# The last 64 rows of w_down on TensorE's row halves in all four token blocks, with the turned rest on the whole array

## The chip, the cores and the metric

The kernel runs on one core of a Trainium2 chip. The metric is the device time of one execution in microseconds (us). TensorE (PE) multiplies matrices into eight banks of PSUM, VectorE (DVE), ScalarE (ACT) and GpSimd (POOL) do the rest, and SP issues the transfers. Each engine works off its own queue in order; a semaphore holds an instruction back until what it needs is there.

## The reference

2048 tokens x of width 640 go through two branches, and a gate per token mixes them. Cut to what matters:

```python
qkv = x @ wqkv                          # 32 heads of 20
pq, pk = q @ w_phi, k @ w_phi           # per head
phi = concat(softmax(p), softmax(-p))   # of pq and of pk
num = phi_q @ (phi_k.T @ v); den = phi_q @ sum(phi_k) + 1e-6
a = (num / den) @ wo
b = (silu(x @ w_gate) * (x @ w_up)) @ w_down      # w_gate, w_up: 640x1728, w_down: 1728x640
g = sigmoid((x * gate_w).sum(-1))
out = g * a + (1 - g) * b
```

The inner width 1728 of branch b is 13 x 128 + 64. The 64 rows left over are the subject of the change.

## The kernel before

**Blocks and steps.** Tokens are cut into 16 tiles of 128 and four blocks (bt 0 to 3) of 512. Branch b goes through a block in 14 steps k (`ffn`, L706): five matmuls of 512 columns for gate and five for up, each into a bank of its own; then `ffn_tail` (L672): ScalarE takes tanh of gate (L699), ScalarE copies up to `us` (L700), VectorE multiplies (L687), GpSimd makes the product (L697) into `hT`, which holds 14 steps of a block, for two blocks in turn. Step 13 has only 64 rows: its gate and its up share the two halves of the partitions of one bank, in one group of matmuls called gu.

**The sums (w_down).** `down` (L906) sums columns 0 to 511 of the result for one token tile: `hT` of a step stands still in the array, `wd` moves, and 14 matmuls of 512 columns add up in one bank. The last 128 columns are summed turned: in `rest` (L871) `wd` stands still, the block's 512 tokens move, 14 matmuls of 512 columns; ScalarE copies that and a transposing DMA turns it back.

**Block 3 is different (EDGE = (3,), L39).** Blocks 0 to 2 treat step 13 like the others: rows 64 to 127 of `hT`'s step 13 are zero (memset, L606), and a whole matmul is spent on 64 rows of use. In block 3, gu is ten matmuls of 256 columns, which lay the first 256 tokens of step 13 on partitions 0 to 63 and the last 256 on partitions 64 to 127 (the tail then works by halves: L676). `wd` has the 64 rows twice, once on each half (L595, L596). An **edge** (`edge`, L839) adds step 13 for all five sums with matmuls of 64 rows, taking the upper and the lower half in turn; the sums themselves have 13 steps. EARLY (L765) says which sums run ahead of the edge (they open their banks, and the edge closes them); for the others the edge opens the banks and the sum closes them. There the turned rest lies in a pair of banks, 256 tokens each, as 26 matmuls of 256 columns.

**Branch a.** Each key tile (`ktile`, L1119; `features`, L1026) multiplies into a pair of banks and one more for values, and VectorE passes over the pair four times (max L1077, min L1081, subtractions L1085 and L1089) before it is free; then exp, a sum, a reciprocal and GpSimd's product (L1110). Each query tile does the same in one bank, and then num, den, a transpose and the matmuls with `wo` (wof, worest: L1224, L1234).

**The order of the work.** `_Plan` (L253) decides it when the kernel is built: each task has an engine, a guessed cost, what it depends on, what it takes (banks and other buffers) and a priority. The planner goes through modelled time, lets each engine take the first task in its list whose needs are met, and writes the instructions in that order. Key tiles (3), query tiles (5), num, wo and worest (1 to 1.6) go ahead of branch b (10 and up). Within branch b the order is the list `seq` (L1268 to L1278): the sums of a block are strewn one by one among the steps of the next block from its sixth on (D_AFTER, L763), or behind them. K_AT, K_EACH, Q_AT and Q_EACH (L758) are the earliest times of key and query tiles. On the chip the written order is kept, whatever the real times are.

Of the kernel before, what the change touches and what calls it, by code (L numbers as in the profile page):

```python
# [38 lines left out]
EDGE = (3,)  # L39
# [318 lines left out]
def _build(  # L358
# [36 lines left out]
    wd = sb("wd", [P, NK, D], BF16)  # L395
    wg = sb("wg", [P, 5, F_FFN + 128], BF16)
# [109 lines left out]

    L_SLACK, E_SLACK, O_SLACK = 1.0, 1.8, 1.6
# [55 lines left out]
    def load_head(key, c0, c1, k0, k1, land, prio):  # L563
        w, src = (wg, gsrc) if key == "g" else (wu, usrc)
        t = load("sp", w[:, c0:c1, k0 * P:k1 * P], src[:, c0:c1, k0 * P:k1 * P], land, prio)
        for k in range(k0, k1):
# [29 lines left out]
            load("sp", wd[64:P, 13, :], B_w_down[13 * P:F_FFN, :], 59.3, -23.9)]  # L596
# [9 lines left out]
    add("dve", 0.5, lambda: memset(hT[64:P, :, 13, :], 0.0, "dve"), prio=-18)  # L606
# [65 lines left out]
    def ffn_tail(bt, k, ctx, last, n_after):  # L672
        hb = bt % 2
        halves = [(0, P, 0, P, slice(0, 512))]
        if k == 13:
            halves = [(r0, r0 + 64, 64 - r0, P - r0, slice(4 * r0, 4 * r0 + 256)) for r0 in (0, 64)] if bt in EDGE else [(0, 64, 64, P, slice(0, 512))]  # L676

        def each(fn):
            def go():
                for r0, r1, u0, u1, tk in halves:  # L680
                    fn(hT[r0:r1, hb, k, 0:tk.stop - tk.start], lambda: one(ctx["g"], 0, 512, r0, r1)[:, tk],
                       lambda: one(ctx["u" if k < 13 else "g"], 0, 512, u0, u1)[:, tk], lambda: us[r0:r1, ctx["us"], 0:tk.stop - tk.start])
            return go

        def stt(h, g, u, s_):
            g_ = g()
            dveop(lambda: dve.scalar_tensor_tensor(out=h, in0=h, scalar=1.0, in1=g_, op0=ALU.add, op1=ALU.mult), [h, g_], [h])  # L687

        def copy(h, g, u, s_):
            o_, u_ = s_(), u()  # L690
            run("act", lambda: act.activation(o_, u_, ACTF.Copy, scale=0.5), reads=[u_], writes=[o_] if k < 13 else [o_, u_])  # L691

        def mult():
            n = 256 if k == 13 and bt in EDGE else 512
            r1 = 64 if k == 13 and bt not in EDGE else P
            h, u_ = hT[0:r1, hb, k, 0:n], us[0:r1, ctx["us"], 0:n]
            poolop(lambda: pool.tensor_tensor(h, h, u_, ALU.mult), [h, u_], [h])  # L697
        x_ = 0.15 if k == 13 and bt in EDGE else 0.0
# [4 lines left out]
        mult_t[bt, k] = add("pool", 0.6 if k == 13 and bt in EDGE else 1.11, mult,  # L703
                            deps=[t2, t3], prio=0, rel=[("us", ctx, "us")], name="hmul")

    def ffn(bt, k, rank):  # L706
# [68 lines left out]

    DM = 512
# [62 lines left out]
    def edge(bt, rank):  # L839
        hb = bt % 2  # L840
        c_ = down_c[bt] = {j: {} for j in range(-1, 4)}
        acq = [("pair" if j < 0 else "bank", c_[j], "ps") for j in range(-1, 4) if j not in EARLY[bt]] + ([("bank", c_[3], "p2")] if bt == NBT - 1 else [])

        def turned(r0):
            return (bank(c_[-1]["ps"], r0 // 64, 0, 256), wd[r0:r0 + 64, 13, DM:D], hT[r0:r0 + 64, hb, 13, 0:256], -1)
# [11 lines left out]
    def body(bt, j, o, pairs):  # L857
        if bt not in EDGE:
            return acc(o(), pairs)
        early = j in EARLY[bt]  # L860
        return [(o(), l, r, early and i == 0, not early and i == 12) for i, (l, r) in enumerate(pairs)]

    def sums(bt, j, cost, fn, rank, acq, name):
        if bt not in EDGE:
            t_ = add("pe", cost, fn, deps=[mult_t[bt, k] for k in range(NK)] + wd_l, prio=rank, acq=acq, name=name)
            return t_, t_
        t_ = add("pe", cost, fn, deps=[mult_t[bt, k] for k in range(13)] + wd_l, prio=rank, acq=acq if j in EARLY[bt] else (), name=name)
        (edge_t[bt] if j in EARLY[bt] else t_).deps.append(t_ if j in EARLY[bt] else edge_t[bt])
        return t_, edge_t[bt] if j in EARLY[bt] else t_

    def rest(bt, rank):  # L871
        ctx = down_c[bt][-1]
# [3 lines left out]
        got = [("pair" if bt in EDGE else "bank", ctx, "ps")]  # L876

        def fn():
            if bt not in EDGE:
                mms(acc(one(ctx["ps"], 0, 512), [(wd[:, k, DM:D], hT[:, hb, k, :]) for k in range(NK)]))  # L880
                return
            mms([g for i in range(2) for g in body(bt, -1, lambda i=i: bank(ctx["ps"], i, 0, 256),
                                                   [(wd[:, k, DM:D], hT[:, hb, k, 256 * i:256 * i + 256]) for k in range(13)])])
        rest_t[bt], r_ = sums(bt, -1, _mm(*([256] * 26 if bt in EDGE else [512] * 14)), fn, rank, got, "rest")

        def rcp():
            if bt not in EDGE:
                actop(xb[:, ctx["xb"], 0:512], one(ctx["ps"], 0, 512), ACTF.Copy)
                return
            i_ = wide(ctx["ps"], 1024).rearrange("p (i x) -> p i x", i=2)[:, :, 0:256]  # L890
            actop(xb[:, ctx["xb"], 0:512].rearrange("p (i x) -> p i x", i=2), i_, ACTF.Copy)
        e = add("act", 0.49, rcp, deps=[r_], prio=1, acq=[("xb", ctx, "xb")], rel=got, name="rcp")
# [13 lines left out]
    def down(bt, u, rank):  # L906
        t = 4 * bt + u
        ctx = down_c[bt][u]
        hb = bt % 2
        tk = slice(P * u, P * u + P)  # L910

        def part(key, c0, c1):
            return lambda: mms(body(bt, u, lambda: one(ctx[key], 0, c1 - c0), [(hT[:, hb, k, tk], wd[:, k, c0:c1]) for k in range(13 if bt in EDGE else NK)]))
        if t < NT - 1:
            down_t[bt, u], d_ = sums(bt, u, _mm(*[DM] * (13 if bt in EDGE else NK)), part("ps", 0, DM), rank, [("bank", ctx, "ps")], "down")
            return t, ctx, [(d_, "ps", 0, DM)]
        assert u not in EARLY[bt]
        first, _ = sums(bt, u, _mm(*[384] * 13), part("ps", 0, 384), rank, (), "down")
        second = add("pe", _mm(*[128] * 13), part("p2", 384, DM), prio=0.0, name="down")
        second.after = first  # L920
        down_t[bt, u] = second
        return t, ctx, [(first, "ps", 0, 384), (second, "p2", 384, DM)]
# [344 lines left out]
    late = downs_of(NBT - 2)[LATE:]  # L1267
    seq = [("f", k, bt) for k in range(K_PAIRS) for bt in range(2) if bt or k >= HD]  # L1268
    seq += [("f", k, 0) for k in range(K_PAIRS, NK)]
    for bt in range(1, NBT):  # L1270
        ks = list(range(K_PAIRS if bt == 1 else 0, NK))
        ds = downs_of(bt - 1)
        for i, k in enumerate(ks):
# [4 lines left out]
    seq = [e for e in seq if e not in late] + late + downs_of(NBT - 1)  # L1278
    downs = []
    for i, (kind, j, bt) in enumerate(seq):  # L1280
        if kind == "f":
            ffn(bt, j, 10.0 + 0.01 * i)
        elif kind == "d":
            if bt in EDGE and bt not in edge_t:
                edge(bt, 10.0 + 0.01 * seq.index(("x", 0, bt)))
            down_c.setdefault(bt, {c: {} for c in range(-1, 4)})
            if j < 0:
                rest(bt, 10.0 + 0.01 * i)
                continue
# [59 lines left out]
```

## Time and profile before

| | us |
|---|---|
| median of 3 runs | 286.55 (286.29 to 286.63) |
| the profiled execution | 286.89 |
| its span, first to last instruction | 285.1 |
| TensorE busy | 282.0, 1695 matmuls |
| VectorE busy | 225.8 |
| GpSimd busy | 168.0 |
| ScalarE busy | 153.2 |

A row of the profile that describes a group names the line, the engine, the operation, the tiles written and read, the shapes and the count; behind the bar stand the busy time of the group in us and the mean of one in ns, and after a second bar the time its engine idled just before, with what ended it. Nearly all matmuls have line L466, since one helper writes them; they are told apart by tiles: `ps<-xT,wg` is gate or gu, `ps<-xT,wu` up, `ps<-wd,hT` a tile's sum, `ps<-hT,wd` the turned rest, `ps<-wo,oT` and `ps<-oT,wo` the last product of branch a. A matmul's recorded length contains its way through the array, so consecutive ones overlap; what one costs in a stream is the distance between two starts. A line of a timeline has the start and the length in us ahead of engine and line.

### The profile page before, as it was taken

The page shows a single profiled execution, that of the slowest core. Times are in us where ns is not written, and L with a number is a line of the kernel's source. Part 1 is how long each engine was busy: PE and PEld are TensorE (multiplying, and loading weights), DVE is VectorE, ACT ScalarE, POOL GpSimd, SP SyncE. Part 2 cuts the span into 40 slices and gives each one's busy share as a digit, 9 for nine tenths or more (in the row PEclk, how much of TensorE's full clock was granted, in tenths as well). Part 3 has the DMA queues.
Part 4 walks back from the last instruction along what each step waited for, and adds up shares of the span by engine and source line. Part 5 has one row for each costly group of instructions (what it writes and reads, how often), then busy time and mean ns, then how long its engine had stood idle before and what let it go on. Part 6 is the DMA issues. An engine that isn't in the chain of part 4 may idle for free.

```text
span 285.1 us, 4487 instructions
## 1 busy us (share of the span) xinstructions
PE 282.0 (99%) x1695; PEld 137.9 (48%) x1695; DVE 225.8 (79%) x330; ACT 153.2 (54%) x266; POOL 168.0 (59%) x140
## 2 busy tenths in 40 slices
PE   8999999999999999999999999999999999999996
PEld 3444544444554445444544554445454444444644
DVE  1323369999899979999999999999999888863213
ACT  2455746776767744566664435547554545435410
POOL 4099713776677674447876953587978584453300
PEclk9999999999999999999999999999999999999999
DMA  7989998942000010000001122452652664653012
GB/s 173 263 127 146 304 220 156 310 133 52 14 16 13 1 39 14 10 14 16 14 17 32 29 49 50 97 65 57 134 153 43 122 159 89 81 107 115 5 37 92
DMA packets 74511, 25.41 MB, mean 89 GB/s; under 512 B 62585, under 2 KB 74489, under 8 KB 74489
## 3 DMA queue, kind: packets, MB, share of 16 engines
q1 hardware_dynamic: 73177, 25.10, 41.6%
q8 instruction: 13, 0.21, 0.3%
q10 hardware_dynamic: 1312, 0.03, 0.3%
q14 instruction: 9, 0.07, 0.1%
HBM read 8.46 MB, written 2.62 MB: 39 GB/s over the span
## 4 chain that ended last, share of the span: by engine, by line
PE 98%; POOL 0%; ACT 0%; issue 0%; DVE 0%; POOLq 0%
PE ps L466 97%; PE ps L646 2%; POOL hT L697 0%; ACT us L691 0%; DVE xsb L801 0%; POOLq L156 0%
## 5 line engine op out<-in xcount | busy, mean ns | idle before, releaser
L697 POOL TENSOR_TENSOR hT<-hT,us 128x512 bf16<-128x512 bf16 (+2 forms) x56 | 63.7, 1146 | 57.6 <-DVE hT L687 31.6
L1110 POOL TENSOR_TENSOR phi<-phi,rc 128x1680 bf16<-128x1680 bf16 (+1 forms) x32 | 77.5, 2425 | 32.8 <-DVE rc L1104 29.8
L466 PE MATMUL ps<-xT,wg 128*128 128x512 bf16 (+1 forms) x285 | 70.0, 379 | 0.0
L466 PE MATMUL ps<-xT,wu 128*128 128x512 bf16 x260 | 64.3, 379 | 0.0
L687 DVE SCALAR_TENSOR_TENSOR hT<-hT,ps 128x512 bf16<-128x512 bf16 (+2 forms) x57 | 37.7, 668 | 31.2 <-ACT hT L476 28.3
L476 ACT ACTIVATE hT<-ps 128x512 bf16<-128x512 f32 (+2 forms) x57 | 33.2, 587 | 36.4 <-PE ps L466 36.0
L466 PE MATMUL ps<-wkv,xT 128*128 128x460 bf16 (+2 forms) x240 | 51.1, 366 | 0.0
L466 PE MATMUL ps<-wd,hT 128*128 128x512 bf16 (+4 forms) x238 | 50.3, 367 | 0.0
L1100 DVE TENSOR_REDUCE sm<-phi 128x84 f32<-128x1680 bf16 (+1 forms) x32 | 48.4, 1513 | 1.2 <-ACT phi L476 1.1
L476 ACT ACTIVATE phi<-phi 128x1680 bf16<-128x1680 bf16 (+1 forms) x32 | 41.6, 1301 | 13.7 <-DVE phi L1089 13.7
L466 PEld LDWEIGHTS ps<-xT,wg 128*128 128x128 bf16 x285 | 27.0, 98 | 30.5 <-issue 2.0
L691 ACT ACTIVATE us<-ps 128x512 bf16<-128x512 f32 (+2 forms) x57 | 33.2, 588 | 14.5 <-PE ps L466 13.2
L466 PEld LDWEIGHTS ps<-xT,wu 128*128 128x128 bf16 x260 | 25.4, 98 | 30.7 <-ACT us L691 0.4
L466 PEld LDWEIGHTS ps<-wkv,xT 128*128 128x128 bf16 x240 | 23.2, 98 | 24.7
L466 PEld LDWEIGHTS ps<-wd,hT 128*128 128x128 bf16 (+1 forms) x238 | 22.3, 98 | 24.7 <-ACT gtan L1009 0.3
L1077 DVE TENSOR_REDUCE mx<-ps 128x42 f32<-128x840 f32 (+1 forms) x32 | 26.5, 830 | 7.5 <-PE ps L466 7.5
L1081 DVE TENSOR_REDUCE mn<-ps 128x42 f32<-128x840 f32 (+1 forms) x32 | 26.7, 835 | 0.0
L1089 DVE TENSOR_TENSOR phi<-mn,ps 128x840 bf16<-128x840 f32 (+1 forms) x32 | 26.3, 823 | 0.4
L1085 DVE TENSOR_TENSOR phi<-ps,mx 128x840 bf16<-128x840 f32 (+1 forms) x32 | 26.1, 815 | 0.0
L466 PE MATMUL ps<-wo,oT 128*128 128x512 bf16 x80 | 19.9, 379 | 0.0
L813 POOL TENSOR_TENSOR xsb<-xsb,xb 128x512 bf16<-128x512 bf16 x12 | 13.9, 1154 | 8.5 <-ACT xb L476 8.5
L466 PE MATMUL ps<-wq,xT 128*128 128x480 bf16 x80 | 18.8, 366 | 0.0
(61 smaller groups left out, 207.2 us busy)
## 6 DMA issues: line engine op xcount, KB each, us to landing
out_dram<-xsb SPq DMA_DIRECT2D x15, 160.0 KB, 1.9
wd<-in_B_w_down_dram SPq DMA_DIRECT2D x1, 2080.0 KB, 10.0
wg<-in_B_w_gate_dram SPq DMA_DIRECT2D x2, 400.0 KB, 5.2
wu<-in_B_w_up_dram SPq DMA_DIRECT2D x2, 400.0 KB, 5.8
wo<-in_A_wo_dram SPq DMA_DIRECT2D x1, 800.0 KB, 5.4
wg<-in_B_w_gate_dram SPq DMA_DIRECT2D x2, 320.0 KB, 4.3
wu<-in_B_w_up_dram SPq DMA_DIRECT2D x2, 320.0 KB, 4.9
wkv<-in_A_wqkv_dram SPq DMA_DIRECT2D x1, 600.0 KB, 5.5
```

Of the source, the lines that this page charges most:

```text
L466: last = pe.matmul(o, lhsT=l, rhs=r, start=st, stop=sp_, skip_group_check=True)
L476: run("act", lambda: act.activation(o, i, func, scale=scale), reads=reads, writes=[o])
L687: dveop(lambda: dve.scalar_tensor_tensor(out=h, in0=h, scalar=1.0, in1=g_, op0=ALU.add, op1=ALU.mult), [h, g_], [h])
L691: run("act", lambda: act.activation(o_, u_, ACTF.Copy, scale=0.5), reads=[u_], writes=[o_] if k < 13 else [o_, u_])
L697: poolop(lambda: pool.tensor_tensor(h, h, u_, ALU.mult), [h, u_], [h])
L813: poolop(lambda: pool.tensor_tensor(x_, x_, b_, ALU.add), [x_, b_], [x_])
L1077: dveop(lambda: dve.tensor_reduce(a, b, AX.X, ALU.max), [b], [a])
L1081: dveop(lambda: dve.tensor_reduce(a, b, AX.X, ALU.min), [b], [a])
L1085: dveop(lambda: dve.tensor_tensor(o_, a, b, ALU.subtract), [a, mx[:, ctx["st"], 0:nh]], [o_])
L1089: dveop(lambda: dve.tensor_tensor(o_, a, b, ALU.subtract), [b, mn[:, ctx["st"], 0:nh]], [o_])
L1100: dveop(lambda: dve.tensor_reduce(a, b, AX.X, ALU.add), [b], [a])
L1110: poolop(lambda: pool.tensor_tensor(a, a, b, ALU.mult), [a, r], [a])
```

## The change

All four blocks are treated as block 3 was, with four differences. The edge contains only the four tiles (in the order 0, 2, 1, 3), not the turned rest. The turned rest runs in one bank on the whole array: 13 matmuls of 512 columns and two of 256 for step 13, one for each half of the tokens; so that a whole-array matmul may read `hT`'s step 13, with its two halves of tokens, one set of weights has zeros in rows 64 to 127 (`wd[64:P, 13, DM:D]`), and a new tile `wr` has zeros in rows 0 to 63 and the 64 rows below. The load of the second copy of those rows is split in two for that. The sums of a block stand together in `seq`: rest after step 1 of the next block, and tiles 0, 1, the edge, tiles 2, 3 after step 2 (for block 1, whose first nine steps run beside block 0's, after its steps 10 and 11). Tiles 0 and 1 are ahead of the edge in every block. The earliest times of key and query tiles and of the products with w_phi move a little.

```diff
-EDGE = (3,)
+    wr = sb("wr", [P, P], BF16)
...
-            load("sp", wd[64:P, 13, :], B_w_down[13 * P:F_FFN, :], 59.3, -23.9)]
+            load("sp", wd[64:P, 13, 0:DM], B_w_down[13 * P:F_FFN, 0:DM], 59.3, -23.9),
+            load("sp", wr[64:P, :], B_w_down[13 * P:F_FFN, DM:D], 59.5, -23.8)]
...
-    add("dve", 0.5, lambda: memset(hT[64:P, :, 13, :], 0.0, "dve"), prio=-18)
+    for z_ in (wd[64:P, 13, DM:D], wr[0:64, :]):
+        wd_l[3].deps.append(add("dve", 0.2, lambda z_=z_: memset(z_, 0.0, "dve"), prio=-18))
...
-            halves = [(r0, r0 + 64, 64 - r0, P - r0, slice(4 * r0, 4 * r0 + 256)) for r0 in (0, 64)] if bt in EDGE else [(0, 64, 64, P, slice(0, 512))]
+            halves = [(r0, r0 + 64, 64 - r0, P - r0, slice(4 * r0, 4 * r0 + 256)) for r0 in (0, 64)]
...
-            gu = add("pe", _mm(*([256] * 10 if bt in EDGE else [512] * 5)), lambda: mms(half(0) + half(1) if bt in EDGE else acc(one(ctx["g"], 0, 512),
-                      [(wg[:, c, 1664:1792], xT[:, c, tsl]) for c in range(5)])),
+            gu = add("pe", _mm(*[256] * 10), lambda: mms(half(0) + half(1)),
...
-    K_AT, K_EACH, Q_AT, Q_EACH = 30.00, 6.744, 137.55, 6.876
-    PRE_Q = 10.14
-    PRE_EACH = 2.2
+    K_AT, K_EACH, Q_AT, Q_EACH = 29.00, 6.821, 136.36, 6.844
+    PRE_Q = 10.07
+    PRE_EACH = 2.0
...
-    D_AFTER = 5
+    D_AFTER = 1
...
-    EARLY = ((), (-1, 0, 1), (-1, 0, 1), (-1,))
-    LATE = 6
+    EARLY = ((0, 1),) * NBT
...
-            order = [turned(0), tile(2), tile(0), last[0], tile(1)] + last[1:] + [turned(64)]
-            mms([(o, l, r, j not in EARLY[bt], j in EARLY[bt]) for o, l, r, j in order])
-        edge_t[bt] = add("pe", 0.95, fn, deps=[mult_t[bt, 13]] + wd_l, prio=rank, acq=acq, name="edge")
+            mms([(o, l, r, u not in EARLY[bt], u in EARLY[bt]) for o, l, r, u in [tile(0), tile(2), tile(1)] + last])
+        edge_t[bt] = add("pe", 0.63, fn, deps=[mult_t[bt, 13]] + wd_l, prio=rank, acq=acq, name="edge")
...
-            mms([g for i in range(2) for g in body(bt, -1, lambda i=i: bank(ctx["ps"], i, 0, 256),
-                                                   [(wd[:, k, DM:D], hT[:, hb, k, 256 * i:256 * i + 256]) for k in range(13)])])
-        rest_t[bt], r_ = sums(bt, -1, _mm(*([256] * 26 if bt in EDGE else [512] * 14)), fn, rank, got, "rest")
+            o = one(ctx["ps"], 0, 512)
+            mms([(o, wd[:, k, DM:D], hT[:, hb, k, :], k == 0, False) for k in range(13)] +
+                [(o[:, 256 * i:256 * i + 256], l, hT[:, hb, 13, 0:256], False, True) for i, l in enumerate((wd[:, 13, DM:D], wr[:, :]))])
+        rest_t[bt] = r_ = add("pe", _mm(*([512] * 13 + [256] * 2)), fn, deps=[mult_t[bt, k] for k in range(NK)] + wd_l, prio=rank,
+                              acq=[("bank", ctx, "ps")], name="rest")
...
-        js = [-1, 0, 1, 2, 3]
-        return [("d", j, bt) for j in js if j in EARLY[bt]] + [("x", 0, bt)] * (bt in EDGE) + [("d", j, bt) for j in js if j not in EARLY[bt]]
+        e = [("d", u, bt) for u in range(4)]
+        return [("r", 0, bt)] + e[0:2] + [("x", 0, bt)] + e[2:]
...
-            if i >= D_AFTER and ds:
-                seq.append(ds.pop(0))
-        seq += ds
+            if k == K_PAIRS * (bt == 1) + D_AFTER:
+                seq += downs_of(bt - 1)[:1]
+            if k == K_PAIRS * (bt == 1) + D_AFTER + 1:
+                seq += downs_of(bt - 1)[1:]
```

More of the change, by code (lines that the diff above doesn't have):

```diff
@@ L505, in _build @@
     v1pad = v1all.rearrange("p (g x) -> p g x", x=WIN)[:, :, WIN - 1]
+    DM = 512
     L_SLACK, E_SLACK, O_SLACK = 1.0, 1.8, 1.6
@@ L840, in edge @@
         hb = bt % 2
[L841 to L845, printed above, removed]
+        c_ = down_c[bt] = [{} for _ in range(4)]
+        acq = [("bank", c_[u], "ps") for u in range(4) if u not in EARLY[bt]] + ([("bank", c_[3], "p2")] if bt == NBT - 1 else [])
         def tile(u, key="ps", c0=0, c1=DM):
@@ L852, in fn @@
             last = [tile(3)] if bt < NBT - 1 else [tile(3, "ps", 0, 384), tile(3, "p2", 384, DM)]
-            order = [turned(0), tile(2), tile(0), last[0], tile(1)] + last[1:] + [turned(64)]
-            mms([(o, l, r, j not in EARLY[bt], j in EARLY[bt]) for o, l, r, j in order])
-        edge_t[bt] = add("pe", 0.95, fn, deps=[mult_t[bt, 13]] + wd_l, prio=rank, acq=acq, name="edge")
[L857 to L869, printed above, removed]
+            mms([(o, l, r, u not in EARLY[bt], u in EARLY[bt]) for o, l, r, u in [tile(0), tile(2), tile(1)] + last])
+        edge_t[bt] = add("pe", 0.63, fn, deps=[mult_t[bt, 13]] + wd_l, prio=rank, acq=acq, name="edge")
     def rest(bt, rank):
-        ctx = down_c[bt][-1]
+        ctx = {}
         rest_c[bt] = ctx
@@ L909, in down @@
         hb = bt % 2
+        early = u in EARLY[bt]
         tk = slice(P * u, P * u + P)
         def part(key, c0, c1):
[L913 to L920, printed above, removed]
+            return lambda: mms([(one(ctx[key], 0, c1 - c0), hT[:, hb, k, tk], wd[:, k, c0:c1], early and k == 0, not early and k == 12) for k in range(13)])
+        n = DM if t < NT - 1 else 384
+        d_ = add("pe", _mm(*[n] * 13), part("ps", 0, n), deps=[mult_t[bt, k] for k in range(13)] + wd_l, prio=rank,
+                 acq=[("bank", ctx, "ps")] if early else (), name="down")
+        down_t[bt, u] = d_
+        if early:
+            edge_t[bt].deps.append(d_)
+            return t, ctx, [(edge_t[bt], "ps", 0, n)]
+        d_.deps.append(edge_t[bt])
+        if n == DM:
+            return t, ctx, [(d_, "ps", 0, n)]
+        second = add("pe", _mm(*[DM - n] * 13), part("p2", n, DM), prio=0.0, name="down")
+        second.after = d_
         down_t[bt, u] = second
-        return t, ctx, [(first, "ps", 0, 384), (second, "p2", 384, DM)]
+        return t, ctx, [(d_, "ps", 0, n), (second, "p2", n, DM)]
     def piece(which, c, m, o_):
@@ L1270, in _build @@
     for bt in range(1, NBT):
[L1271 to L1273 removed]
+        for k in range(K_PAIRS if bt == 1 else 0, NK):
             seq.append(("f", k, bt))
[L1275 to L1278 removed]
+            if k == K_PAIRS * (bt == 1) + D_AFTER:
+                seq += downs_of(bt - 1)[:1]
+            if k == K_PAIRS * (bt == 1) + D_AFTER + 1:
+                seq += downs_of(bt - 1)[1:]
+    seq += downs_of(NBT - 1)
     downs = []
@@ L1282, in _build @@
             ffn(bt, j, 10.0 + 0.01 * i)
+        elif kind == "r":
+            rest(bt, 10.0 + 0.01 * i)
         elif kind == "d":
-            if bt in EDGE and bt not in edge_t:
+            if bt not in edge_t:
                 edge(bt, 10.0 + 0.01 * seq.index(("x", 0, bt)))
[L1286 to L1289, printed above, removed]
             downs.append(down(bt, j, 10.0 + 0.01 * i))
```

23 lines of the change are left out of this document (6 added, 17 removed).

## The prediction

> **What bounds the kernel now.** I read the page first (busy time, slices, chain), then the start times of the matmuls in the timeline, then the forms of the instructions that the change makes more or fewer of.
>
> The page, its first, second and fourth part:
>
> ```profile
> PE 282.0 (99%) x1695; PEld 137.9 (48%) x1695; DVE 225.8 (79%) x330; ACT 153.2 (54%) x266; POOL 168.0 (59%) x140
> ...
> PE   8999999999999999999999999999999999999996
> ...
> PEclk9999999999999999999999999999999999999999
> ...
> PE 98%; POOL 0%; ACT 0%; issue 0%; DVE 0%; POOLq 0%
> ```
>
> TensorE is busy in every slice at full granted clock, and the chain that ended last is 98% TensorE. Busy time alone can hide gaps, because the recorded matmuls overlap (379 ns each for 512 columns), so I took the distance from each start to the next: 216 ns for 512 columns, 109 for 256, 162 for 384, 56 for 128. After the warm-up only four distances are more than 20 ns too long without a reason in the shapes: 0.06 us at 30.74, 0.07 at 64.04, 0.08 at 174.97 and 0.27 at 266.36, 0.48 us together. So the time is the sum of TensorE's distances plus what lies before the first and behind the last matmul. A nanosecond less of matmul is a nanosecond less of time, as long as no new wait opens.
>
> The timeline of TensorE around the one edge of now (block 3):
>
> ```profile
> 270.55 0.38 PE L466 MATMUL ps<-oT,wo 128*128 128x512 bf16 x1
> 270.86 0.28 PE L466 MATMUL ps<-hT,wd 64*128 64x256 bf16 x1
> 270.87 0.71 PE L466 MATMUL ps<-wd,hT 64*128 64x512 bf16 x5
> 271.31 0.27 PE L466 MATMUL ps<-hT,wd 64*128 64x256 bf16 x1
> 271.51 0.39 PE L466 MATMUL ps<-wd,hT 128*128 128x512 bf16 x1
> ```
>
> The second and third line start 4 ns apart: the row halves do run side by side. Columns 1 and 2 are start and length, so the price can be read off: the matmul at 270.552 should hand over at 270.768, but the edge starts at 270.863 (95 ns lost); its seven matmuls are 1280 columns in each half and last to 271.418 (555 ns); the next whole-array matmul starts at 271.512 (94 ns lost). Together 0.744 us.
>
> **The change on TensorE.** Blocks 0 to 2, each:
> - The four tile sums lose their 14th matmul: 4 x 216 = -0.864 us.
> - An edge comes: 1024 columns a half instead of 1280, so 555 - 107 = 448, plus 95 and 94: +0.637.
> - gu of step 13: ten of 256 for five of 512: 1090 - 1080 = +0.010.
> - rest: 13 x 216 + 2 x 109 for 14 x 216: +0.002.
>
> That is -0.215 a block, -0.645 for three. Block 3: rest goes from 26 x 109 = 2.834 to 13 x 216 + 2 x 109 = 3.026, +0.192; its edge loses the two turned matmuls, 0.744 to 0.64 (tile 3 stays split), -0.104; together +0.088. **Sum: -0.56 us.**
>
> A drain at each change of tiling mode is what the Trainium skill, "TensorEngine Tiling (Array Packing)", Key Properties, states; the 95 and 94 ns agree. "TensorE: Matmul & The Clock Gate", Single matmul latency, gives a warm matmul (398 + N)/2.4 ns, as the 379 ns for 512 columns here, so a full drain would cost some 166 ns each way (an estimate from the page); the sum by that is about -0.13 us instead of -0.56.
>
> **The change elsewhere.** By form, mean ns behind the count and busy time:
>
> ```profile
> L697 POOL TENSOR_TENSOR hT<-hT,us 64x512 bf16<-64x512 bf16 x3 | 3.5, 1150 | 3.2 <-DVE hT L687 3.2
> L687 DVE SCALAR_TENSOR_TENSOR hT<-hT,ps 64x512 bf16<-64x512 bf16 x3 | 2.0, 673 | 0.3 <-ACT us L691 0.3
> L691 ACT ACTIVATE us<-ps 64x512 bf16<-64x512 f32 x3 | 1.8, 595 | 0.1
> ...
> L687 DVE SCALAR_TENSOR_TENSOR hT<-hT,ps 64x256 bf16<-64x256 bf16 x2 | 0.8, 419 | 2.5 <-ACT us L691 2.5
> L691 ACT ACTIVATE us<-ps 64x256 bf16<-64x256 f32 x2 | 0.8, 380 | 0.1
> ...
> L697 POOL TENSOR_TENSOR hT<-hT,us 128x256 bf16<-128x256 bf16 x1 | 0.7, 671 | 1.5 <-DVE hT L687 1.5
> ```
>
> Per block 0 to 2, ScalarE gets four of 380 for two of about 592 (+0.34), VectorE two of 419 for one of 673 (+0.17), GpSimd 671 for 1150 (-0.48). The tail of step 13 becomes about 0.15 us longer: halves start 0.41 apart, so four of them 1.65, then 0.84 and 0.67, 3.16 against 1.19 + 0.67 + 1.15 = 3.01. What hides it: rest now stands behind two gate and up pairs of the next block, 4.3 us. Without that cover it is at most what the queues made of it so far: from the last gu matmul to the end of the product 4.7, 5.1 and 3.6 us, so up to 0.8 us in block 1; I take nothing, since feature work lies between too. Behind a rest or an edge that waits stands all of TensorE's queue, tiles 2 and 3 first, and ScalarE's copies of the sums behind them. VectorE, 20.0 of 20 us busy in the stretches 40 to 60 and 80 to 100, gets 0.5 us more in all; its cover is at the end, 13.6 of 20 us in 240 to 260 (busy time by stretches). At the start one VectorE memset of 485 ns (64x512) goes and two smaller ones come (between 59 ns for 2 elements a partition and 485), while VectorE has nothing to do; SP issues one more load (465 to 1009 ns for those of wd now, no more bytes in all) behind wd's and ahead of wo's, at about 59 us, and wo is first read at 179.6. GpSimd's queue is moved past nothing else. All this at nothing; the bound is 0 to 0.5 us if the queue of SP holds up a turn of features then.
>
> The sums move: rest and tiles of a block now come together after steps 1 and 2 of the next one, not spread from step 5. The work is the same; the four tiles, though, hold banks longer, below.
>
> The end decides one more wait. TensorE, then GpSimd:
>
> ```profile
> 264.40 1.25 PE L466 MATMUL ps<-xT,wg 128*128 128x256 bf16 x10
> 265.50 1.24 PE L466 MATMUL ps<-wo,oT 128*128 128x512 bf16 x5
> 266.84 0.61 PE L466 MATMUL ps<-hT,wd 128*128 128x256 bf16 x4
> ```
>
> ```profile
> 265.63 1.15 POOL L697 TENSOR_TENSOR hT<-hT,us 128x512 bf16<-128x512 bf16 x1 [1.29 <-ACT us L691]
> ```
>
> The first sum of block 3 waits for the product of step 12 (ends 266.78). Gu (1.09) and one wo group (1.08) fill 2.17 of the 2.44 us; 0.27 is left. The same wait stands ahead of tile 0 after the change, with rest behind it, so step 13's product has two tiles of cover. With another wo or worest group there it is gone; with none it is 1.35 us.
>
> **The number.** The profiled execution took 286.89 us (span 285.1 and 1.8 around it): 286.89 - 0.56 = 286.33. It lies 0.34 above the median of the runs, 286.55; so 285.99, **286.0 us**.
>
> **Rivals.**
> 1. The waits go as well: 286.0 - 0.3 to 0.5 = 285.5 to 285.7. For it: the query tiles may start 1.2 to 1.7 us earlier (Q_AT, Q_EACH), so both last wo groups can be ready for the end. Against: a new order brings waits of its own.
> 2. The other side, **banks at the edge**. The edge needs two free banks at once while tiles 0 and 1 hold two. A key tile holds a pair from its first matmul to its last subtraction: the one begun at 101.93 is let go at 111.95, as this view of VectorE shows, and the next has begun at 108.69:
>
> ```profile
> 109.86 1.02 DVE L1085 TENSOR_TENSOR phi<-ps,mx 128x840 bf16<-128x840 f32 x1
> 110.92 1.03 DVE L1089 TENSOR_TENSOR phi<-mn,ps 128x840 bf16<-128x840 f32 x1
> ```
>
> So 4 of 8 banks are often with keys, two with tiles, and one more with values or kv leaves too few. If the edges of blocks 0 and 1 each wait for one such subtraction, 2 x 1.0 us: 286.0 + 2.0 = 288.0. Block 2's lies among query tiles, one bank each. From 0.3 us a block on the gain is gone. Against it: gate and up steps can fill, if they find banks.
> 3. The end wait loses its cover (the wo group comes too early): +1.08, 287.1.
> 4. The edge costs more amid the blocks than at the end, each next matmul waiting for the recorded end of the last: 270.931 against 270.863, 0.07 more, twice, in three blocks: +0.4, 286.4. The two gaps measured speak against it. It is where the Trainium skill's single-matmul latency (above) would lead.
> 5. It does not do what it says: halves one after the other would be +3 x 0.43, 287.3. The 4 ns exclude it for these shapes.
>
> **How the numbers follow.** Forecast 47% (own range 285.6 to 286.5), rival 1 15%, rival 2 20%, rival 3 11%, rival 4 6%, rival 5 1%. A fifth of a per cent is 0.57 us, about what a measurement of this kernel can tell from no change; its lower bound, 285.98, cuts the forecast in two. Faster: 24 + 15 = 39%. Same: 23 + 6 of rival 3 + 6 = 35%. Slower: 20 + 5 + 1 = 26%. The range goes from 285.3 to 288.0: it holds every case but the upper half of rival 2 (three edges late, or longer waits) and what none of them names.
>
> **What would show it.** Right: 15 matmuls of 64x512, each of the first three edges 0.64 us with gaps of 95 ns at both ends, 13 matmuls a tile, no idle time of TensorE beyond 0.5 us in all, VectorE and ScalarE hardly changed. Wrong: a distance of more than 0.3 us ahead of an edge or a rest (rival 2, or step 13's product late), an idle time above 0.3 us at the last block's first sum (rival 3), gaps at edges near 0.17 us (rival 4), or an end behind the last matmul other than the 2.2 us of now.

## The result, and the profile after

The changed kernel takes **286.06 us** (median of 22 runs, 285.59 to 286.56). The kernel before took 286.46 (286.04 to 287.01, 22 runs) beside it. The ratio is 0.9985, with a 95% interval of 0.9978 to 0.9991: faster by 0.15%, or 0.40 us. The forecast was 286.0, from a change of -0.56 us. The profiled execution took 285.67 us, its span 284.0.

The page of the changed kernel, its first, second and fourth part:

```profile
PE 279.0 (98%) x1671; PEld 137.1 (48%) x1700; DVE 226.5 (80%) x334; ACT 153.3 (54%) x272; POOL 166.8 (59%) x140
...
PE   8999999999999999999999999999999999999996
...
PEclk9999999999999999999999999999999999999999
...
PE 89%; DVE 8%; issue 1%; ACT 1%; POOL 0%; POOLq 0%
```

Nothing here tells that the kernel is faster. The 3.0 us that TensorE's busy time fell by are mostly no gain: 1700 weights were loaded, but only 1671 matmuls are recorded, so 29 records are missing, and each leaves a distance that is one matmul too long. A second profile of the same code (e9, below) has all 1700 records and 281.2 us. The chain shows more: it has gone from 98% TensorE to 89%, with 8% on VectorE. A chain follows each wait back to what released it, and where TensorE now waits for VectorE, it goes along VectorE's queue for several microseconds, although the wait itself lasts a fraction of one. So the percentage tells that there is a new wait, not what it costs; e9 has the same wait, and there the chain is 96% TensorE and 2% VectorE.

What it costs is in the distances between starts. I divided each span in three: up to the first gate matmul of step 4 (start), from there to the start of the last matmul (stream), and from there to the end (tail). Waits are what the distances in the stream have beyond what the shapes, the changes between 128 and 64 rows (changes of mode) and the missing records explain.

| us | start | stream | of it waits | stream without waits | tail |
|---|---|---|---|---|---|
| before | 14.55 | 268.18 | 0.46 | 267.72 | 2.41 |
| after | 13.76 | 267.77 | 0.61 | 267.16 | 2.41 |
| difference | -0.79 | -0.41 | +0.15 | **-0.56** | 0.00 |

The matmuls became shorter by 0.56 us, the sum of the prediction; the waits took back 0.15. That leaves -0.41, and the medians differ by 0.40.

**The start is no part of the gain.** It makes two thirds of the 1.22 us between the two profiled executions. The changed kernel was profiled once more as e9, from the same code. First the changed kernel, then e9, the first eight gate matmuls:

```profile
4.97 1.89 PE L466 MATMUL ps<-xT,wg 128*128 128x512 bf16 x8
```

```profile
5.27 2.33 PE L466 MATMUL ps<-xT,wg 128*128 128x512 bf16 x8
```

The second column is the length of the whole group. At first the starts are 427 ns apart, then 216; the first execution reached the short distance at 4.97 us, e9 at 6.36, the kernel before at 6.77. So e9's start is 14.34 where that of the same code was 13.76, while its stream is 267.78 against 267.77. The waits for the first loads differ by execution too: e1 reached the short distance at 5.16 us, but it waits 0.54 us for `wg` further on, and its start is 14.51. Whoever compares two profiled spans must take the start out first.

**The edges.** The timeline of TensorE around the edge of block 2:

```profile
149.41 0.97 PE L466 MATMUL ps<-wq,xT 128*128 128x480 bf16 x4
150.32 0.61 PE L466 MATMUL ps<-wd,hT 64*128 64x512 bf16 x4
150.85 0.82 PE L466 MATMUL ps<-xT,wg 128*128 128x512 bf16 x3
```

Four matmuls of 64 rows lie in 0.61 us: the starts are 150.317 and 150.320, then 150.543 and 150.547. With the gaps at both ends the four edges cost 0.646, 0.634, 0.633 and 0.636 us (0.637 predicted); behind the first a record is missing, and e9, which has it, gives 0.635 there. The gaps are 95 to 97 ns going in and 92 to 93 coming out (102 at the missing record), and nothing waits ahead of any edge.

**The two waits that count.** The first is at 81.36 us, in block 0's turn. VectorE, then TensorE:

```profile
76.71 0.87 DVE L690 SCALAR_TENSOR_TENSOR hT<-hT,ps 64x256 bf16<-64x256 bf16 x2
77.61 0.68 DVE L1084 RECIPROCAL rc<-sm 128x84 f32<-128x84 f32 x1
78.32 1.03 DVE L1065 TENSOR_TENSOR phi<-ps,mx 128x840 bf16<-128x840 f32 x1
79.27 1.02 DVE L1057 TENSOR_REDUCE mx<-ps 128x42 f32<-128x840 f32 x1
80.21 0.48 DVE L1138 COPY kvacc<-ps 128x320 f32<-128x320 f32 x1
80.61 1.02 DVE L1069 TENSOR_TENSOR phi<-mn,ps 128x840 bf16<-128x840 f32 x1
```

```profile
80.28 1.24 PE L466 MATMUL ps<-xT,wu 128*128 128x512 bf16 x5
81.69 1.55 PE L466 MATMUL ps<-wkv,xT 128*128 128x460 bf16 x7 [0.16 <-DVE phi L1069]
```

Five up matmuls from 80.28 hand over at 80.28 + 5 x 0.216 = 81.36; the key tile begins at 81.69, when the subtraction that frees its pair of banks has ended (81.63). That is 0.33 us. (The profile writes 0.16, since a matmul's recorded length overlaps its successor.) Further up in VectorE's queue stand the two halves of step 13's product, 0.87 us, where before one instruction of 0.67 stood. But two other things changed there. Before, two pairs of gate and up stood ahead of this key tile, which began at 83.98, long after the same subtraction had ended (80.87 + 1.01 = 81.88); with the changed order and planned times it is one pair. And the max pass of the next key tile (L1057, 1.02 us) now stands ahead of that subtraction, where before it stood behind. The experiments e7, e11 and e12 take these apart.

The second is the wait of before at the last block's first sum, on TensorE and on GpSimd:

```profile
263.13 1.25 PE L466 MATMUL ps<-xT,wg 128*128 128x256 bf16 x10
264.50 0.82 PE L466 MATMUL ps<-wd,hT 128*128 128x512 bf16 x3
```

```profile
263.30 1.15 POOL L699 TENSOR_TENSOR hT<-hT,us 128x512 bf16<-128x512 bf16 x1 [2.71 <-ACT us L694]
```

The sum starts 1.37 us after gu, which takes 1.09: 0.28 are idle (0.27 before), until the product of step 12 ends at 264.45. One wo group stands between, as before.

### The profile page after: what moved, and what is told of

It reads as the page before. It is cut to its first block, busy times and chain, and to the rows that moved or that the text cites. A ratio compares the mean times of both kernels' runs of the same rounds, so it can differ in the third digit from the quotient of the medians.

```text
span 284.0 us, 4497 instructions
## 1 busy us (share of the span) xinstructions
PE 279.0 (98%) x1671; PEld 137.1 (48%) x1700; DVE 226.5 (80%) x334; ACT 153.3 (54%) x272; POOL 166.8 (59%) x140
## 4 chain that ended last, share of the span: by engine, by line
PE 89%; DVE 8%; issue 1%; ACT 1%; POOL 0%; POOLq 0%
PE ps L466 87%; PE ps L649 2%; DVE sm L1080 1%; DVE mx L1057 1%; DVE hT L690 1%; DVE phi L1065 1%; DVE phi L1069 1%; DVE ob L1192 1%; DVE mn L1061 1%; DVE rc L1084 1%; ACT us L694 0%; POOL hT L699 0%; ACT hT L476 0%; DVE rd L1184 0%; DVE dn L1182 0%
## 5 line engine op out<-in xcount | busy, mean ns | idle before, releaser
L699 POOL TENSOR_TENSOR hT<-hT,us 128x512 bf16<-128x512 bf16 (+1 forms) x56 | 62.4, 1121 | 61.9 <-DVE hT L690 35.4
L466 PE MATMUL ps<-xT,wg 128*128 128x512 bf16 (+1 forms) x285 | 65.9, 364 | 1.0 <-issue 0.2
L690 DVE SCALAR_TENSOR_TENSOR hT<-hT,ps 128x512 bf16<-128x512 bf16 (+1 forms) x60 | 38.4, 645 | 27.9 <-ACT hT L476 24.1
L476 ACT ACTIVATE hT<-ps 128x512 bf16<-128x512 f32 (+1 forms) x60 | 33.8, 567 | 36.4 <-PE ps L466 36.2
L466 PE MATMUL ps<-wd,hT 128*128 128x512 bf16 (+3 forms) x231 | 48.3, 366 | 0.3
L466 PEld LDWEIGHTS ps<-xT,wg 128*128 128x128 bf16 x300 | 28.1, 98 | 29.2 <-issue 1.4
L694 ACT ACTIVATE us<-ps 128x512 bf16<-128x512 f32 (+1 forms) x60 | 33.9, 568 | 13.9 <-PE ps L466 12.8
L466 PEld LDWEIGHTS ps<-wd,hT 128*128 128x128 bf16 (+1 forms) x238 | 21.3, 98 | 25.1 <-issue 1.0
L1057 DVE TENSOR_REDUCE mx<-ps 128x42 f32<-128x840 f32 (+1 forms) x32 | 26.7, 833 | 7.6 <-PE ps L466 7.4
L476 ACT ACTIVATE xb<-ps 128x512 bf16<-128x512 f32 x16 | 9.5, 595 | 19.7 <-PE ps L466 19.7
L466 PE MATMUL ps<-wo,oT 128*128 128x512 bf16 x77 | 19.2, 379 | 0.1
```

Of the source, the lines that this page charges most:

```text
L466: last = pe.matmul(o, lhsT=l, rhs=r, start=st, stop=sp_, skip_group_check=True)
L476: run("act", lambda: act.activation(o, i, func, scale=scale), reads=reads, writes=[o])
L1057: dveop(lambda: dve.tensor_reduce(a, b, AX.X, ALU.max), [b], [a])
```

## The experiments

The kernel before, measured beside them, took 286.45 us (beside e1 to e4), 286.23 (e5 to e8) and 286.5 (e9 to e12); each of the three series ran on another chip, so medians of different series are compared by the ratio or by the stream. The theory: the time follows the sum of TensorE's distances, and what it misses are waits for VectorE and GpSimd. The rivals: the new order of sums, keys and queries is what brings or takes the time; the edge's price depends on how it is written; banks or a semaphore decide it.

| run | median us | ratio to before (95%) | stream | tail |
|---|---|---|---|---|
| e1 edge on the whole array | 286.86 | 1.0010 (1.0000 to 1.0019) | 268.65 | 2.41 |
| e2 one half after the other | 286.06 | 0.9979 (0.9970 to 0.9988) | 267.83 | 2.42 |
| e3 no edges | 284.24 | 0.9909 (0.9894 to 0.9924) | 266.04 | 2.42 |
| e4 old order | 287.59 | 1.0030 (1.0017 to 1.0043) | 267.39 | 4.40 |
| e5 edges alone | 347.82 | 1.2148 (1.2132 to 1.2165) | | |
| e6 last block's first sum split | 285.71 | 0.9979 (0.9970 to 0.9989) | 267.49 | 2.41 |
| e7 old order, last turn early | 285.71 | 0.9983 (0.9974 to 0.9992) | 267.41 | 2.65 |
| e8 edge ahead of all tiles | 293.31 | 1.0253 (1.0235 to 1.0272) | 274.86 | 2.41 |
| e9 the changed kernel again | 285.96 | 0.9984 (0.9976 to 0.9993) | 267.78 | 2.41 |
| e10 edge in two visits | 286.72 | 1.0010 (1.0002 to 1.0019) | 268.73 | 2.42 |
| e11 e6, and block 0's halves later | 285.49 | 0.9968 (0.9956 to 0.9980) | 267.32 | 2.41 |
| e12 one half left out | 285.52 | 0.9972 (0.9962 to 0.9981) | 267.42 | 2.42 |

**e1, the four tiles' step 13 on the whole array.**

```diff
-hT[r0:r0 + 64, hb, 13, ...], wd[r0:r0 + 64, 13, c0:c1]
+hT[:, hb, 13, ...], wd[:, 13, c0:c1]
```

> The changed kernel with the edges' matmuls on all 128 rows instead of 64 (one matmul of 512 columns a tile, so each tile also gets the product of the other half's token tile, which does not belong there). The order of all engines is that of the changed kernel. Theory (the time is TensorE's sum, and the gain of the change is that the halves run side by side): an edge becomes 4 x 0.216 = 0.864 us instead of 0.636, no gaps at its ends, so +0.23 in four blocks, +0.91: 286.06 to 287.0, slower than the kernel before by 0.5. Rival A (the gain came from the new order and earlier starts, not from the halves): 286.1, as the changed kernel. Rival B (VectorE sets the pace and TensorE has slack): 286.1 too, with new idle time of TensorE elsewhere gone.

The stream is 0.88 us longer than that of the change, the median 0.80. The timeline of TensorE at the same edge shows 1.03 where 0.61 was, and 0.86 instead of 0.53 from this start to that of the next group (152.04):

```profile
151.18 1.03 PE L466 MATMUL ps<-wd,hT 128*128 128x512 bf16 x4
```

So the gain of the change is that of the row halves: without them the stream is 0.47 us longer than that of the kernel before (268.65 against 268.18).

**e2, both upper matmuls written ahead of both lower ones.**

```diff
-[tile(0), tile(2), tile(1)] + last
+[tile(0), tile(1), tile(2)] + last
```

> The changed kernel with the edge's tiles in the order 0, 1, 2, 3 instead of 0, 2, 1, 3: two matmuls of the upper half, then two of the lower. Theory: matmuls start in order, so tile 1 waits for tile 0, tile 2 runs beside tile 1, tile 3 waits for tile 2: three times 216 ns instead of two, +0.215 us an edge, +0.86 in all: 286.9. If the halves did not need to alternate (the two lower ones run beside the two upper ones): 286.1. Rival B (slack on TensorE): 286.1.

```profile
150.69 0.61 PE L466 MATMUL ps<-wd,hT 64*128 64x512 bf16 x4
151.24 0.60 PE L466 MATMUL ps<-xT,wg 128*128 128x512 bf16 x2
```

Nothing changed: TensorE's timeline has the same 0.61 us, and the starts are 150.694, 150.701, 150.921 and 150.927, again in pairs. My expectation of a matmul's distance more in each edge failed. The program had the order upper, upper, lower, lower. Records do not name the half, so that is an inference: if the first two records were both of the upper half, 1024 columns would have run in it within the time that 512 take (216 ns), and then the same in the lower half. So the third must have run ahead of the second, and within such an edge TensorE's queue was not worked off in order. The Trainium skill, "TensorE: Matmul & The Clock Gate", Part 3 (packing small matmuls), says that matmuls keep strict order; this run contradicts it for matmuls of different row halves.

**e3, no edges.** The step of 64 rows is left out of the four tile sums.

```diff
-            mms([(o, l, r, ...) ... in [tile(0), tile(2), tile(1)] + last])
+            pass
```

> The changed kernel without the edges' matmuls: step 13's share of the tile sums is left out (that of the turned rest stays). The order of all other instructions is the same. Theory: 4 x 0.636 us go, -2.54: 283.5, if no new wait opens. Rival B (VectorE is nearly as busy as TensorE and holds it back): the first 1 us is given back as waits for VectorE or for banks, 284.5 or more.

The edges' four times 0.64 us went out of the matmuls, but the stream fell by 1.73 only. Its waits are 1.45 us instead of 0.61: new ones of 0.17, 0.30 and 0.38 at 109.6, 162.2 and 244.3. They end with VectorE (`kvacc`), with ScalarE (`us`) and with a transposing DMA (`oT`). So a third of what TensorE saves here is given back to engines that did not become faster with it.

**e4, the sums strewn and the planned times as before.**

```diff
-    K_AT, K_EACH, Q_AT, Q_EACH = 29.00, 6.821, 136.36, 6.844
+    K_AT, K_EACH, Q_AT, Q_EACH = 30.00, 6.744, 137.55, 6.876
...
+            if i >= D_AFTER and ds:
+                seq.append(ds.pop(0))
+        seq += ds
```

> The changed kernel with the sums strewn one by one from the next block's sixth step on and the earliest times of key and query tiles of the kernel before; the edges and the turned rest stay as changed. Theory: the same sum of TensorE, so 286.0 to 286.2, unless its waits differ from the changed kernel's 0.6 us by what the trace will show. Rival A (the order made the gain): 286.46 or more, as before.

It is slower than the change by 1.53 us, and than before by 0.3%. But its stream is 0.38 shorter than that of the change; all of the loss lies behind the last matmul, 4.40 instead of 2.41. VectorE and SP at the end of e4:

```profile
280.94 0.62 DVE L799 SCALAR_TENSOR_TENSOR xsb<-ps,gs,xsb 128x384 bf16<-128x384 f32 x1 [1.36 <-PE ps L466]
281.48 0.34 DVE L818 SCALAR_TENSOR_TENSOR xsb<-rX,gs,xsb 128x128 bf16<-128x128 bf16 x1
281.74 0.34 DVE L799 SCALAR_TENSOR_TENSOR xsb<-ps,gs,xsb 128x128 bf16<-128x128 f32 x1
282.00 0.86 DVE L818 SCALAR_TENSOR_TENSOR xsb<-rX,gs,xsb 128x128 bf16<-128x128 bf16 x3
```

```profile
281.58 2.76 SPq L494 DMA_DIRECT2D out_dram<-xsb  x6
```

Four small additions (L818) stand at the very end of VectorE's queue, though VectorE had been idle for 1.36 us, and the six last stores are issued only from 281.58 on. In the changed kernel SP's line is

```profile
277.75 4.77 SPq L494 DMA_DIRECT2D out_dram<-xsb  x6
```

so the same six begin 3.83 us earlier there. The planner believed that the last turn (the transposing DMA behind the rest) would end later, and wrote the additions behind tile 15's sum.

**e7, e4 with the last turn planned earlier**, the order on TensorE being the same as in e4:

```diff
-        x_.slack = E_SLACK
+        x_.slack = E_SLACK if bt < NBT - 1 else 0.0
```

> e4_old_order with one number of the planner changed: the last block's turned rest of branch a is taken to land 1.8 us earlier. TensorE's order is the same; VectorE adds the four turned pieces ahead of the last but one sum of tile 15 instead of around the last, and the stores follow. Theory: what e4_old_order lost lies behind TensorE's last matmul (4.4 us from its start to the end of the span instead of 2.5), so 1.9 us come back: 285.7, below the changed kernel, since its TensorE waits are 0.4 us less. Rival A (the order of the sums costs 1.1 us amid the kernel): 287.4 or more.

The tail is 2.65 instead of 4.40 and the time 285.71: 1.75 us of tail went with no matmul moved. The order in one piece is therefore not what makes the matmuls of the change cheaper; with its planned times it costs 0.36 us in the stream (267.77 against 267.41), and it leaves the end as short as it was before. All of the 0.36 are waits: those of e7 are about 0.25 us where the change has 0.61, and without them both streams are 267.16.

e7 also shows where the change's wait of 0.33 us comes from. VectorE has the same two halves (0.86 us, from 77.32) in its queue, and the same subtraction ends at 81.70, but the key tile begins 1.67 us later, without a wait. VectorE, then TensorE:

```profile
80.68 1.02 DVE L1069 TENSOR_TENSOR phi<-mn,ps 128x840 bf16<-128x840 f32 x1
```

```profile
82.29 1.24 PE L466 MATMUL ps<-xT,wu 128*128 128x512 bf16 x5
83.37 0.94 PE L466 MATMUL ps<-wkv,xT 128*128 128x460 bf16 x4
```

So two halves instead of one product do not make the wait by themselves. It opens where the changed order and planned times put the key tile one gate and up pair (2.16 us) nearer to that subtraction.

**e5, edges in all blocks on the kernel before**, with its own rest and order:

```diff
-EDGE = (3,)
+EDGE = (0, 1, 2, 3)
```

> The kernel before with edges in all four blocks (EDGE = (0, 1, 2, 3)) and nothing else: its order, its turned rest in the row halves and in a pair of banks. Theory (TensorE's sum): per block 0 to 2 the rest becomes 26 x 109 instead of 14 x 216 (-0.19), the tiles -0.864, the edge +0.744, gu +0.01, so -0.30, three times -0.90: 285.56, if the waits and the end stay. Rival 2 (banks: the pair of the rest and the tiles' banks are held at once) gives waits of more than 0.9 us in all ahead of rests or edges: 286.5 or more. Rival A (the order decides, not TensorE's sum): no faster than before either.

It takes 347.82 us. This is no fair test of the edge. Block 0's entry of EARLY is empty, so its edge needs a pair and four more banks at once. The planner puts it off to 276.36 us, behind the edges of blocks 1 (109.63) and 3 (174.75), and block 2's gate and up run at 295 to 325, since the buffer of `hT` they need is block 0's. The busy times by stretches, in the order of the columns PE, PEld, DVE, ACT, POOL, granted clock:

```profile
180.00:200.00 20.00, 10.67 (x57) 4.44 (x55) 18.37 (x33) 4.62 (x5) 5.96 (x5) 0.67 0.34 66
200.00:220.00 20.00, 10.72 (x63) 4.77 (x64) 19.00 (x36) 3.60 (x4) 9.65 (x6) 0.65 0.49 94
```

What it shows is that with the rest and the EARLY of the kernel before, block 0's edge comes too late; it does not show what an edge is worth there. Block 0 with early sums, and all else as before, was not tried.

**e8, no tile sum ahead of the edge**, so that the edge takes four banks at once:

```diff
-    EARLY = ((0, 1),) * NBT
+    EARLY = ((),) * NBT
```

> The changed kernel with EARLY empty in all blocks: the edge comes ahead of all four tile sums and takes four banks at once. Theory: TensorE's sum is the same, so 286.1, give or take 0.3 for other waits. Rival 2 (banks at the edge): TensorE waits 0.5 us or more ahead of each of the first two edges, 287 to 288.

The stream is 7.09 us longer, the gaps at the edges unchanged (95 and 92 ns). Nor does TensorE wait ahead of an edge. The time went to eight smaller new waits of 0.15 to 1.77 us and to one at the end:

```profile
270.68 1.24 PE L466 MATMUL ps<-oT,wo 128*128 128x512 bf16 x5
274.19 1.04 PE L466 MATMUL ps<-hT,wd 128*128 128x512 bf16 x4 [2.28 <-POOL hT L699]
```

The last block's rest comes before the tiles here and waits 2.44 us (274.195 - 270.677 - 5 x 0.2158) for the product of step 13, which the two early tiles hide in the change. The two longest of the smaller waits (1.33 and 1.77 us) stand ahead of up matmuls and end with VectorE's instructions that read PSUM (L1192, L690). So an edge that takes four banks costs microseconds, but by way of the planner's order, not as the wait at the edge that I had written; how much of it is a wait for a bank was not taken apart.

**e9, the changed kernel once more, and e10, the edge in two visits**, with tile 1's matmul of step 12 between the two pairs:

```diff
-            mms([... in [tile(0), tile(2), tile(1)] + last])
+            mms(g[0:2] + [between] + g[2:])
```

> The changed kernel once more, on the chip and among the runs of e10 to e12, so that they can be compared with it directly. All theories: 286.0 to 286.1, 0.15% under the kernel before.

> The changed kernel with each edge cut in two visits to the row halves: tiles 0 and 2, then one whole-array matmul (tile 1's step 12, taken from the end of its sum), then tiles 1 and 3. The work is the same, one more change into the halves and back an edge. Theory (a change costs 95 and 94 ns each way, as at every edge so far, beside matmuls of 216): from 0.636 to 2 x 0.406 = 0.81 beside the matmul between, +0.18 an edge, +0.7 in all: 286.8. If the gaps were waits for semaphores (banks, step 13's product) and not the change itself: one gap only per edge, 286.1.

e9 repeats stream and waits (0.33 and 0.28 us) of the change. e10's stream is 0.95 longer than e9's; 0.12 of that is a wait in block 0 that the change did not have, so 0.83 are four more pairs of gaps, about 0.2 each. TensorE at block 2's edge, all five matmuls in one line:

```profile
150.48 1.03 PE L466 MATMUL ps<-wd,hT 64*128 64x512 bf16 x5
151.45 0.61 PE L466 MATMUL ps<-xT,wg 128*128 128x512 bf16 x2
```

The gaps are 95 to 97 ns into the first pair, 102 out of it, 107 into the second, 93 to 102 out. No semaphore is waited for in the middle of the edge, and the gaps there are as long as at its ends: the price is that of the change of mode.

**e6, the last block's first sum in two tasks**, twelve steps and then the thirteenth, so that only the last matmul waits for the product of step 12:

```diff
+            d1 = add("pe", _mm(*n12), some(range(12)), deps=[mult_t[bt, k] for k in range(12)] + wd_l, ...)
+            d_ = add("pe", _mm(n), some((12,)), deps=[mult_t[bt, 12]], ...)
```

> The changed kernel with block 3's first tile sum cut in two tasks, steps 0 to 11 and step 12, so that TensorE can begin before step 12's product is there. All orders are the same. Theory: the wait of 0.28 us ahead of that sum goes (steps 0 to 11 are 2.6 us, and the product is 0.3 us late), nothing else moves: 285.8. Rival: the wait comes back at the rest, which needs step 13's product (it ends 0.7 us ahead of the rest now): 286.0.

The wait of 0.28 us is gone and the stream is 0.28 shorter: the end wait is worth its length. The median is 0.35 lower, but the kernel before was 0.23 lower in this series too, so the median says no more than that.

**e12, one half of step 13's product on VectorE left out in block 0** (the last 256 tokens of block 0 lack that factor), and **e11, e6 with both halves later in VectorE's queue**, by a lower priority:

```diff
-        t3 = add("dve", ..., prio=0, ...)
+        t3 = add("dve", ..., prio=2.9 if (bt, k) == (0, 13) else 0, ...)
```

> The changed kernel with the second VectorE half of block 0's step 13 left out (the last 256 tokens of block 0 lack a factor there); nothing else is changed. Theory: VectorE is done 0.42 us earlier at the key tile's passes, so TensorE's wait at 81.7 falls from 0.33 to 0.0: 285.7. Rival as in e11: 286.06.

> e6_split_first_sum with block 0's step 13 set behind the key tile's work in VectorE's order (its two halves of 64x256 come 3 instructions later). TensorE's order is the same. Theory (the wait of 0.33 us ahead of a key tile at 81.7 comes from VectorE, whose two halves of 0.87 us stand ahead of the passes that free the key's banks, where one instruction of 0.67 stood before): the wait falls to 0.1 or less, 285.4 to 285.5. Rival (the bank is late for another reason, the product or ScalarE): the wait stays, 285.7.

In e12 the wait of 0.33 is gone and the stream 0.35 shorter. In e11 nothing is left out. VectorE, then TensorE:

```profile
78.33 0.86 DVE L690 SCALAR_TENSOR_TENSOR hT<-hT,ps 64x256 bf16<-64x256 bf16 x2
79.22 1.03 DVE L1076 TENSOR_TENSOR phi<-mn,ps 128x840 bf16<-128x840 f32 x1
80.16 0.48 DVE L1145 COPY kvacc<-ps 128x320 f32<-128x320 f32 x1
80.56 1.02 DVE L1064 TENSOR_REDUCE mx<-ps 128x42 f32<-128x840 f32 x1
```

```profile
80.55 1.24 PE L466 MATMUL ps<-xT,wu 128*128 128x512 bf16 x5
81.63 1.54 PE L466 MATMUL ps<-wkv,xT 128*128 128x460 bf16 x7
```

The subtraction that frees the banks (L1076 here) now ends at 80.25, and the key tile follows the up matmuls without a gap (80.55 + 1.08 = 81.63). A wait of 0.16 comes at 184.0 instead. But the halves still stand ahead of that subtraction. What went from ahead of it to behind it are the max pass of the next key tile and a copy, since the planner wrote the queue anew. So e11 shows that VectorE's order alone can take the wait away; it does not show, as I had meant it to, that the halves make it, and that its time came out as expected is luck. The stream is 0.46 shorter than e9's and the median 0.47: 285.49 us, ratio 0.9968, the fastest kernel of this study that computes everything.

## Why the prediction was right

**The sum on TensorE was right to 0.01 us**: -0.56 predicted, -0.56 found once the waits are taken out, in the change and, with another order, in e7. The edge cost 0.635 of 0.637 predicted, and e1 confirms the price of the alternative: +0.88, where four edges of four whole matmuls for 0.637 make 4 x (0.864 - 0.637) = +0.91.

**The waits were taken as unchanged and grew by 0.15.** Three small ones of before (0.20 together) went, the end wait stayed as forecast (0.27 to 0.28), and one of 0.33 came. What the prediction had at nothing is the sum of two things, which it names apart: "VectorE ... gets 0.5 us more in all; its cover is at the end", and "a new order brings waits of its own". VectorE is 20.0 of 20 us busy in the stretch from 80 to 100, as the prediction says of before, and slack 150 us later does not help there. e12 shows by taking work out, and e11 by another order, that VectorE's queue ahead of that subtraction sets the wait where the key tile stands now. But two halves add only 0.2 us to that queue (0.87 - 0.67), e12 takes out about 0.41, in e11 the halves stay ahead, and in e7 they make no wait where the key tile begins later. So of the 0.33 us the longer product explains 0.2 at most (an estimate), and the rest comes with the new order: the key tile's earlier place, and the max pass ahead of the subtraction. How those two share it is not shown.

**The 0.34 us by which the profiled execution of before lay above its median** were taken off as a whole, and rightly: 286.89 - 0.41 - 0.34 = 286.14, and 286.06 was measured. Part of it may lie in the start, which differed by 0.58 us between two executions of the changed kernel.

**Some of the closeness is luck.** The forecast of 286.0 is 0.06 us off, but the change that it forecast, -0.56, is 0.16 off, since 0.40 was measured. The kernel before was 286.46 in these runs, not the 286.55 that the forecast starts from, and that made up 0.09 of it. The range from 285.3 to 288.0 holds the time of the kernel before as well, so to lie in it says little. And 0.40 us is less than the fifth of a per cent that the prediction draws as its line, so by that line the time is the same, which had 35%, and not faster, which had 39%.

**The rivals.** The first, that the waits go as well, did not happen, but e11 shows that most of what it promised was there: 285.49 lies at its lower end. The second, banks, did not happen either; EARLY with two tiles is why, since e8 without them loses 7 us, only not ahead of the edges, as the rival has it. The third, a lost cover at the end, is not seen in the change; e8 has one, for step 13's product ahead of the rest (2.44 us). The fourth, dearer edges amid the blocks, falls: 92 to 102 ns at all eight ends, and e10 gives the same without a semaphore. With it falls the estimate of some 166 ns from the Trainium skill, "TensorE: Matmul & The Clock Gate", Single matmul latency, while the drain that "TensorEngine Tiling (Array Packing)", Key Properties, states agrees. The fifth, halves in turn, is excluded by e1 and even by e2, where the written order asks for it.

By form, the VectorE and TensorE groups that the prediction named, mean ns behind the busy time:

```profile
L690 DVE SCALAR_TENSOR_TENSOR hT<-hT,ps 64x256 bf16<-64x256 bf16 x8 | 3.3, 411 | 3.8 <-ACT us L694 3.6
...
L466 PE MATMUL ps<-wd,hT 64*128 64x512 bf16 x15 | 2.4, 382 | 0.0
```

Fifteen edge matmuls of 512 columns are there (the sixteenth tile is split), and eight halves of 411 ns, 419 in the prediction. The sums lie in one piece, each tile of 13, and the end behind the last matmul is that of before, 2.41 us from its start (the 2.2 of the prediction count from its recorded end). Of the signs of being wrong none came: the one distance above 0.3 us, 0.33, lies ahead of a key tile, not of an edge or a rest. Of the signs of being right one is missing: idle time is 0.61 us, not below 0.5.

**What stays open**: why the three small waits of before went, and whether the sums in one piece or the planned times for keys and queries (K_AT and the others) moved the key tile and the max pass; e4 and e7 put back both at once.

## What to carry to other kernels

Where one engine is packed, add up the distances between its starts, edit by edit, and compare stream with stream: the result is good to hundredths of a microsecond, while two whole spans differ by more than the effect because of the start alone. What the sum misses is found on the engine that is nearly as full: look at which release stands behind each instruction added there, and whether the order brings the matmul that needs the release nearer to it, since slack elsewhere in the kernel does not help. And where a planner writes the queues, look at the end of each queue after a change of order; 2 us can lie there with no matmul moved.

## What the runs showed of the hardware

- Matmuls of 64 rows in different row halves do not keep the written order (e2, inferred from the starts): upper, upper, lower, lower ran as two pairs, the starts in a pair 6 to 7 ns apart, 0.61 us in all as when written in turn.
- A change between matmuls of 128 and of 64 rows costs 92 to 107 ns each way, at each edge of the change, e8 and e10, with a semaphore there or without one.
- The short distance of matmuls came between 4.2 (e11) and 6.8 us (before) after the span's start, and differed by 1.4 us between two executions of the same code (4.97 and 6.36). Their starts differ by 0.58 us, of which the first eight gate matmuls, 0.44 us longer in one, are the larger part.
- In e5 the granted clock was 0.67 and 0.65 in the stretches 180 to 200 and 200 to 220, where TensorE is 10.7 of 20 us busy.
